# A preLN block (dilated attention, then a gMLP) rewritten: two token streams, 64-row tile pairs, GELU from table, a list-scheduled order

**Chip, cores, metric.** One core of a Trainium2 chip. The metric is device time in microseconds (us) of one execution. Each kernel ran four times on its chip, beside the kernel before; medians are quoted with their range.

## The reference, cut

```python
# x: [1, 2048, 448] bf16; 16 heads of 28; F = 1792, Fh = 896
def A(x, wqkv, wo):            # attention of 8 keys: positions s, s-2, ..., s-14
    q, k, v = split(x @ wqkv)
    logits = einsum(q, k[s - 2*j]) * 28**-0.5     # j = 0..7, masked below 0
    return (softmax(logits) @ v) @ wo
def B(x, w_in, w_sp, b_sp, w_out):
    z = gelu_tanh(x @ w_in)                       # [2048, 1792]
    z1, z2 = z[..., :896], layernorm(z[..., 896:])
    g = w_sp @ z2 + b_sp[:, None]                 # the "spatial" product, 2048 x 2048
    return (z1 * g) @ w_out
h  = x + A(layernorm(x), wqkv, wo)
h2 = h + B(layernorm(h), w_in, w_sp, b_sp, w_out)
```

## The kernel before

Contractions over 448 run as four passes of 112 rows. Attention takes tiles of 114 queries by 128 keys, of which the mask keeps every second key in a band. The GELU is built from arithmetic and a sigmoid, and the layernorms wait for all 16 blocks.

```python
def issue(self, exe, fn, reads=(), writes=(), prod=None, inc=1):
    ...                            # waits from what the resources hold
    self.ops[exe].append((waits, fn, prod, inc))   # EVERY instruction increments
...
def logits_block(b):               # 16 heads; four 32-row tiles side by side
    for g in range(4):
        for hh in range(4):
            iss("pe", lambda e, ...: e.matmul(out_ap, kT[hh*32:(hh+1)*32, g, t0:t0+nk],
                                qT[hh*32:(hh+1)*32, g, t0+PAD:t0+PAD+nq],
                                tile_position=(hh * 32, 0)), ...)
...
class GeluTile:                    # per 448 or 512 columns
    def copy(self):                # ACT: PSUM -> XB
        ... e.activation(self.XB, self.in_ps_ap, AF.Copy)
    def front(self):               # DVE x3
        ... e.tensor_tensor(self.WK, self.XB, self.XB, ALU.mult)
        ... e.tensor_scalar(self.WK, self.WK, GELU_C, 1.0, ALU.mult, ALU.add)
        ... e.tensor_tensor(self.WK, self.WK, self.XB, ALU.mult)
    def tanh(self):                # ACT
        ... e.activation(self.TB, self.WK, AF.Sigmoid, scale=GELU_K2)
    def back(self):                # DVE, with the row sum for z2
        ... e.tensor_tensor_reduce(self.out_dst_ap, self.TB, self.XB, 1.0, 0.0, ALU.mult, ALU.add, self.sum_x_ap)
    def sq(self):                  # ACT: sum of squares for the layernorm of z2
        ... e.activation(junk2[:, 0:self.n], self.out_dst_ap, AF.Square, accum_out=self.sum_sq_ap)
...
mean_var_from_sums(...); rstd3 = rsqrt_chain(...)   # after ALL 16 blocks of z2
for m in range(NB): ...                             # then normalise all of z2
```

The softmax here doesn't subtract the row's maximum and nothing guards it: scores larger than these inputs give would overflow.

## Time and profile before

| before | value |
|---|---|
| time, median (range) of the three runs the prediction had | 343.62 us (343.18 to 344.04) |
| time, median of the four runs beside the changed kernel | 343.83 us (343.18 to 344.11) |
| profiled span, mean granted TensorE clock | 342.4 us, 0.915 |
| busy: PE, DVE, ACT | 287.6, 242.8, 156.8 us |

The prediction shows the busy line, the slices and the stages. One more view: the page's costliest groups. Columns: line, engine, operation, output and input, shapes, count, then busy us, mean ns of one, and the idle time before with what ended it. These five lines are the arithmetic GELU, with 60 tiles each except the last, which is the 32 of z2:

```profile
L708 ACT ACTIVATE xb<-psum 128x448 bf16<-128x448 f32 (+1 forms) x60 | 33.4, 558 | 108.3 <-PE psum L755 95.5
...
L712 DVE TENSOR_TENSOR wk<-xb 128x448 bf16<-128x448 bf16 (+1 forms) x60 | 24.2, 404 | 40.1 <-ACT xb L708 40.1
...
L718 ACT ACTIVATE tb<-wk 128x448 bf16<-128x448 bf16 (+1 forms) x60 | 35.9, 598 | 12.7 <-DVE wk L714 12.7
...
L714 DVE TENSOR_TENSOR wk<-wk,xb 128x448 bf16<-128x448 bf16 (+1 forms) x60 | 24.5, 408 | 2.1
...
L723 DVE CUSTOM_DVE_ANT_0 z2p<-tb,xb 128x448 bf16<-128x448 bf16 x32 | 19.8, 618 | 0.9 <-ACT tb L718 0.8
```

A tile passes back and forth between ACT and DVE: 33.4 + 35.9 us of ACT and some 97 of DVE (with L713, 17.1, and L727, 11.7, not shown).

### The profile page before, as it was taken

The page shows a single profiled execution, that of the slowest core. Times are in us where ns is not written, and L with a number is a line of the kernel's source. Part 1 is how long each engine was busy: PE and PEld are TensorE (multiplying, and loading weights), DVE is VectorE, ACT ScalarE, POOL GpSimd, SP SyncE. Part 2 cuts the span into 40 slices and gives each one's busy share as a digit, 9 for nine tenths or more (in the row PEclk, how much of TensorE's full clock was granted, in tenths as well). Part 3 has the DMA queues.
Part 4 walks back from the last instruction along what each step waited for, and adds up shares of the span by engine and source line. Part 5 has one row for each costly group of instructions (what it writes and reads, how often), then busy time and mean ns, then how long its engine had stood idle before and what let it go on. Part 6 is the DMA issues. An engine that isn't in the chain of part 4 may idle for free.

```text
span 342.4 us, 4998 instructions
## 1 busy us (share of the span) xinstructions
PE 287.6 (84%) x1859; PEld 144.9 (42%) x1872; DVE 242.8 (71%) x670; ACT 156.8 (46%) x320; POOL 5.1 (1%) x17
## 2 busy tenths in 40 slices
PE   3789899999998848966550099999999999999996
PEld 1434455555565617521110034444444444444442
DVE  4987446897779779899999896554555565545554
ACT  1435878777866020899999322221222022212220
POOL 5000000000000000000000000000000000000000
PEclk9879989999987556999996589999999999999999
DMA  7999900000000069930000000001000100000001
GB/s 223 258 220 179 190 16 2 2 0 2 3 2 1 2 162 187 161 76 0 0 1 1 0 2 0 0 2 50 3 3 0 38 17 0 0 26 30 1 0 54
DMA packets 40537, 16.39 MB, mean 48 GB/s; under 512 B 34177, under 2 KB 39617, under 8 KB 40514
## 3 DMA queue, kind: packets, MB, share of 16 engines
q1 hardware_dynamic: 40514, 16.08, 22.5%
q8 instruction: 14, 0.23, 0.3%
q14 instruction: 9, 0.07, 0.1%
HBM read 5.85 MB, written 1.84 MB: 22 GB/s over the span
## 4 chain that ended last, share of the span: by engine, by line
PE 66%; DVE 28%; ACT 2%; issue 2%; DMA 1%; ACTq 0%; DVEq 0%
PE psum L800 29%; PE psum L383 9%; PE psum L755 7%; PE psum L823 6%; DVE z2p L723 5%; PE psum L400 4%; PE psum L485 4%; PE psum L444 4%; DVE wk L714 3%; DVE wk L712 3%; DVE wk L713 3%; DVE xhT L369 2%; DVE tring L351 2%; PE psum L416 2%; DVE st L347 1%
## 5 line engine op out<-in xcount | busy, mean ns | idle before, releaser
L708 ACT ACTIVATE xb<-psum 128x448 bf16<-128x448 f32 (+1 forms) x60 | 33.4, 558 | 108.3 <-PE psum L755 95.5
L800 PE MATMUL psum<-wspT_lo,z2p 128*128 128x512 bf16 x217 | 52.7, 388 | 17.9 <-DVE z2p L787 17.4
L712 DVE TENSOR_TENSOR wk<-xb 128x448 bf16<-128x448 bf16 (+1 forms) x60 | 24.2, 404 | 40.1 <-ACT xb L708 40.1
L800 PE MATMUL psum<-wspT_hi,z2p 128*128 128x512 bf16 x218 | 49.7, 379 | 0.3
L423 ACT ACTIVATE E<-psum 128x456 bf16<-128x456 f32 (+1 forms) x72 | 39.6, 550 | 15.1 <-PE psum L472 8.8
L800 PEld LDWEIGHTS psum<-wspT_lo,z2p 128*128 128x128 bf16 x224 | 21.9, 98 | 46.9 <-DVE z2p L787 22.3
L718 ACT ACTIVATE tb<-wk 128x448 bf16<-128x448 bf16 (+1 forms) x60 | 35.9, 598 | 12.7 <-DVE wk L714 12.7
L744 PE MATMUL psum<-w_in,xhT 112*128 112x448 bf16 x128 | 28.7, 365 | 11.1 <-ACT xb L708 11.1
L800 PEld LDWEIGHTS psum<-wspT_hi,z2p 128*128 128x128 bf16 x224 | 21.9, 98 | 26.5
L755 PE MATMUL psum<-xhT,w_in 112*128 112x512 bf16 x112 | 28.8, 379 | 1.2 <-ACT xb L708 1.2
L714 DVE TENSOR_TENSOR wk<-wk,xb 128x448 bf16<-128x448 bf16 (+1 forms) x60 | 24.5, 408 | 2.1
L744 PEld LDWEIGHTS psum<-w_in,xhT 112*128 112x128 bf16 x128 | 11.4, 101 | 28.0 <-ACT xb L708 19.0
L444 PEld LDWEIGHTS psum<-V,E 128*114 128x114 bf16 (+1 forms) x288 | 21.4, 149 | 2.4 <-issue 0.4
L823 PE MATMUL psum<-w_out,z1p 128*128 128x448 bf16 x112 | 22.0, 353 | 0.1
L444 PE MATMUL psum<-V,E 128*114 128x29 bf16 (+1 forms) x288 | 21.7, 210 | 0.0
L485 PE MATMUL psum<-wo,OT 112*128 112x448 bf16 x64 | 18.4, 420 | 3.9 <-DVE OT L475 2.8
L432 DVE TENSOR_TENSOR E<-E,maskb 128x1824 bf16<-128x1824 bf16 (+1 forms) x18 | 19.9, 1103 | 1.8 <-ACT E L423 1.7
L813 DVE TENSOR_TENSOR ub<-psum,bb 128x512 bf16<-128x512 f32 x28 | 19.1, 683 | 2.3 <-PE psum L800 2.3
L723 DVE CUSTOM_DVE_ANT_0 z2p<-tb,xb 128x448 bf16<-128x448 bf16 x32 | 19.8, 618 | 0.9 <-ACT tb L718 0.8
L383 PE MATMUL psum<-xhT,wqp 112*128 112x512 bf16 x64 | 18.1, 440 | 2.3 <-DVE xhT L369 2.3
L827 DVE TENSOR_TENSOR tring<-psum,x_tm 128x448 bf16<-128x448 f32 x16 | 10.0, 624 | 13.5 <-PE psum L823 13.5
L713 DVE TENSOR_SCALAR wk<-wk 128x448 bf16<-128x448 bf16 (+1 forms) x60 | 17.1, 285 | 2.1
(82 smaller groups left out, 338.1 us busy)
## 6 DMA issues: line engine op xcount, KB each, us to landing
x_tm<-in_A_x_dram SPq DMA_DIRECT2D x4, 448.0 KB, 7.2
out_dram<-tring SPq DMA_DIRECT2D x16, 112.0 KB, 1.7
w_in<-in_B_w_in_dram SPq DMA_DIRECT2D x1, 1568.0 KB, 15.5
stg<-in_A_wqkv_dram SPq DMA_DIRECT2D x1, 1176.0 KB, 9.9
w_out<-in_B_w_out_dram SPq DMA_DIRECT2D x1, 784.0 KB, 4.5
wo<-in_A_wo_dram SPq DMA_DIRECT2D x1, 392.0 KB, 12.9
wspT_lo<-in_B_w_sp_dram SPq DMA_TRANSPOSE x16, 4.0
wspT_hi<-in_B_w_sp_dram SPq DMA_TRANSPOSE x16, 4.1
```

The lines of the kernel that those rows point to most:

```text
L383: e.matmul(out_ap, wsrc[:, c, gg, :], xhT[0:DC, c, col0:col0 + 512], start=(c == 0), stop=(c == NCH - 1)),
L423: iss("act", lambda e, in_ap=in_ap, out_e=out_e: e.activation(out_e, in_ap, AF.Exp, scale=SCALE), reads=[r_bank[hh]], writes=[r_E[slot]])
L444: e.matmul(psum[0:nq, ob + h * 32: ob + h * 32 + DH + 1], E[0:nk, slot, eidx, 0:nq], V1[0:nk, vslot, h, 0:DH + 1]),
L708: iss("act", lambda e: e.activation(self.XB, self.in_ps_ap, AF.Copy), reads=[self.rbank], writes=[r_xb[s]])
L712: iss("dve", lambda e: e.tensor_tensor(self.WK, self.XB, self.XB, ALU.mult), reads=[r_xb[s]], writes=[r_wk[s]])
L714: iss("dve", lambda e: e.tensor_tensor(self.WK, self.WK, self.XB, ALU.mult), reads=[r_wk[s], r_xb[s]], writes=[r_wk[s]])
L718: iss("act", lambda e: e.activation(self.TB, self.WK, AF.Sigmoid, scale=GELU_K2), reads=[r_wk[s]], writes=[r_tb[s]])
L723: iss("dve", lambda e: e.tensor_tensor_reduce(self.out_dst_ap, self.TB, self.XB, 1.0, 0.0, ALU.mult, ALU.add, self.sum_x_ap), reads=[r_tb[ ...
L744: iss("pe", lambda e, c=c: e.matmul(out_ap, xhT[0:DC, c, PAD + 128 * m: PAD + 128 * m + 128], w_in[:, c, FH + D * k: FH + D * (k + 1)], st ...
L755: iss("pe", lambda e, c=c: e.matmul(out_ap, w_in[:, c, fc * 128:(fc + 1) * 128], xhT[0:DC, c, PAD + 512 * tc: PAD + 512 * (tc + 1)], start ...
L800: iss("pe", lambda e, sbk=sbk: e.matmul(out_ap, z2p[:, sbk, fc * 128:(fc + 1) * 128], wsrc[:, sbk, coff:coff + 512], start=(sbk == 0), sto ...
L823: iss("pe", lambda e, fc=fc: e.matmul(out_ap, z1p[:, fc, 128 * m:128 * m + 128], w_out[:, fc, :], start=(fc == 0), stop=(fc == FC7 - 1)), ...
```

## The change

The intent: fewer PE passes, no arithmetic GELU, and no stage in which PE waits for row statistics. Tokens 0..1023 lie on partitions 0..63 and tokens 1024..2047 on 64..127, so a contraction over 448 is seven passes of 64 rows for both streams, as tile pairs. Attention is split by parity (every second position), so a tile is 64 keys by 58 queries with a narrow band. Row sums are matmuls against ones, their reciprocal is exp of minus log on ACT. The reciprocal root is POOL's power, unit by unit. A list scheduler in the kernel, with estimated durations, fixes each engine's order; the exp and log of attention and the GELU alternate in six table phases.

```diff
 # matmuls of the contractions, here q/k: the two streams as 64-row tiles
+for c in range(NC7):
+    for s in range(2):
+        iss("pe", lambda e, ...: e.matmul(psum[:, bk[s]*512 + ...],
+            wp[64*s:64*s+64, c, cb:cb+128], xh[64*s:64*s+64, c, off+t0:off+t0+cw], ...))
-for c in range(NCH):
-    iss("pe", lambda e, ...: e.matmul(out_ap, wsrc[:, c, gg, :], xhT[0:DC, c, col0:col0+512], ...))
 # logits of one attention tile: 64 small matmuls, eight tiles of the array at a time
+for sg in range(8):
+    s, g = sg // 4, sg % 4
+    for w in range(2):                       # parity
+        for hh in range(4):
+            iss("pe", lambda e, ...: e.matmul(
+                psum[64*w:64*w+64, lb[hh]*512 + sg*JW : ... + JW],
+                kT[32*hh:32*hh+32, s, g, a+w:a+w+127:2],
+                qT[32*hh:32*hh+32, s, g, a+w:a+w+2*JW-1:2],
+                tile_position=(32*hh, 64*w)), ...)
 # (weighted V: likewise 64 matmuls of 64x32 tiles)
 # GELU
+iss("act", lambda e: e.activation(z2p[:, b, :]..., pair_view(zb, 2*s, D), AF.Gelu_apprx_tanh, accum_out=...))
-... copy / front / tanh / back as above
 # reciprocal root of a unit's variance
+iss("pool", lambda e: e.tensor_scalar(dst, var, EPS, None, ALU.add), ...)
+iss("pool", lambda e: e.tensor_tensor(dst, dst, nh, ALU.pow), ...)
 # order
+EPOCHS = [SET_E, SET_G, SET_E, SET_G, SET_E, SET_G]
+EP_TILE[i] = 0 if i < 4 else (2 if i < 7 else 4)     # attention tiles
+EP_UNIT[u] = 1 if u < 2 else (3 if u < 5 else 5)     # z2 units
+pl = Planner({"ps": range(8), "tr": range(NTR), "E": range(NE), ...}, EPOCHS, table_task)
+w_in, wsp loads: issued from the start, in order, on one queue
```

## The prediction

> **What bounds the kernel now.** I read the page's busy line and its 40 slices first, to see whether one engine carries the whole span.
>
> ```profile
> PE 287.6 (84%) x1859; PEld 144.9 (42%) x1872; DVE 242.8 (71%) x670; ACT 156.8 (46%) x320; POOL 5.1 (1%) x17
> ...
> PE   3789899999998848966550099999999999999996
> ...
> DVE  4987446897779779899999896554555565545554
> ACT  1435878777866020899999322221222022212220
> ```
>
> It doesn't: PE is full in slices 5 to 14 and from 23 on, but from 14 to 22 (120 to 195 us) it is half idle while DVE and ACT read 9. So I cut the span by stage (columns: length, then busy us and instructions of PE, PEld, DVE, ACT, POOL, then granted clock, DMA share, GB/s).
>
> ```profile
> 0.00:14.50 14.50, 7.60 (x28) 3.01 (x28) 9.17 (x33) 4.00 (x7) 5.06 (x17) 1.00 0.91 238
> 14.50:36.00 21.50, 18.70 (x97) 9.47 (x98) 17.85 (x62) 10.08 (x18) 0.00 (x0) 0.84 1.03 203
> 36.00:122.00 86.00, 79.81 (x882) 49.43 (x881) 61.62 (x141) 56.96 (x107) 0.00 (x0) 0.87 0.10 18
> 122.00:136.00 14.00, 8.53 (x70) 6.61 (x70) 13.28 (x51) 2.39 (x4) 0.00 (x0) 0.62 0.98 202
> 136.00:196.00 60.00, 30.35 (x136) 11.85 (x135) 55.03 (x189) 53.12 (x131) 0.00 (x0) 0.87 0.24 37
> 196.00:342.40 146.40, 142.59 (x651) 64.57 (x663) 85.86 (x199) 30.28 (x54) 0.00 (x0) 0.99 0.04 13
> ```
>
> Start; first q/k; attention (PE); the second layernorm as a barrier (DVE 13.3 of 14.0); the z2 half of the GELU (DVE 55.0 and ACT 53.1 of 60, PE half idle: there a tile takes four DVE passes and three of ACT); then z1, the spatial product and the output product, PE 142.6 of 146.4. The wait list shows what the layernorm of z2 then costs, one wait of PE for the normalised tensor, and the chain shows the pure PE rhythm afterwards:
>
> ```profile
> PE psum L800 <- DVE z2p L787: 17.4, 1, 17.4
> ```
>
> ```profile
> 202.38 0.87 PE psum L755 x4
> 203.25 3.46 PE psum L800 x16
> ```
>
> 16 matmuls of 512 columns in 3.46 us are 216 ns each, back to back.
>
> **What the Trainium skill says.** "TensorE: Matmul & The Clock Gate", section Back-to-back issue gap, gives N/2.4 + 2.5 ns at full clock; 216 ns for 512 columns agrees, and the 112-row matmuls above (L755, 0.87 us for four) take no less. So a contraction of 448 costs four passes of 112 rows now, and seven half passes of 64 rows, if two run side by side, cost 3.5. The same page, Part 3 (Packing small matmuls), says tiles in different row groups run together, some 4 ns apart. The trace agrees for 32-row tiles (columns: start, us, engine):
>
> ```profile
> 62.46 0.38 PE L416 MATMUL psum<-qT,kT 32*128 32x114 bf16 x16
> 62.77 0.41 PE L472 MATMUL psum<-ident,otm 114*112 114x114 bf16 x4
> ```
>
> 16 logits matmuls take 0.31 us to the next group's start, 19 ns each; alone they would be 114/2.4 + 2.5 = 50. 64-row pairs are shown by no run yet. "ScalarE: Activation LUTs", sections on what happens in an ACTIVATE and What ACT_TABLE_LOAD costs, gives 186 + 0.833 N ns for every function (the 456-column exp here took 551 ns, formula 566), so one GELU from table costs what one copy does, and 1283 ns a table load plus about 1380 of drain. The load is here too, 1283 ns, but the chain puts it at 139.06 and the next ACTIVATE at 140.35: no drain. "TensorEngine Tiling (Array Packing)", Key Properties, says a change of tiling mode drains the array; no view of the kernel before isolates this, so I treat it as a risk.
>
> **The change part by part.** *PE.* At full clock, columns/2.4 + 2.5 ns, the kernel before needs: q/k 128x216 = 27.6 us; V 72x189 = 13.6; attention output product 64x189 = 12.1; z2 128x189 = 24.2; z1 112x216 = 24.2; spatial 448x216 = 96.8; output 112x189 = 21.2; transposes 128x56 + 72x50 = 10.8; logits 288x19 = 5.6; weighted V 288x52 (8 in 0.39 us in the timeline, weights loads of 114 columns) = 15.1. Sum 251.2. After: q/k 7x4x(1024+1038) columns in 280 pair steps = 24.8; V 63 steps = 11.9; attention output unchanged 12.1; z2 112 pair steps 21.2; z1 98 = 21.2; spatial 96.8; output 21.2; transposes 231, two side by side, 6.5; per attention tile of 114 queries and both streams, logits 64 and weighted V 64 matmuls of 58 columns in eights, which I put at 0.6 each (8 steps of 25 to 75 ns), and row sums 0.25, so 9x1.45 = 13.1. Sum 228.8: 22 us less. No transposes of the attention output are left.
>
> *DVE*, with 155 ns + 1.04 per fp32 PSUM element (512 took 683, 448 took 624): LN1 17x0.81 + 16x0.32 + evictions 8x0.61, about 24.5; k evictions 8304 columns in 9 pieces 10.1; mask 9x1.12 (1824 elements took 1.105) = 10.1; attention scaling 9x1.10 = 9.9 (before 0.62+0.26+0.39 for each of 18); residual 8x1.09 = 8.7; LN2 23.4; statistics of z2 for six blocks 8.6; normalising z2 16x0.506 = 8.1; then gate 28x(0.683+0.424) = 31.0 and output 10.0. Sum 144, against 242.8. *ACT*: repack 5.0, q 8.3, V 8.4, exp 18x0.96 = 17.3, reciprocal as log and exp 17.3, z2 GELU 16.8 with its sums, squares of ten blocks 10x1.12 = 11.2, z1 GELU 14x1.04 = 14.5, six table loads 7.7: 107, against 157.
>
> *Barriers.* Row statistics now go block by block, with the power on POOL, so LN2, z2 and its layernorm are woven into attention. What lies there before z1 may start: PE 87 us, DVE 103, ACT 92. z1 and the spatial product are released when the last attention tile's exponentials are done, T8. Of the work before that, some 18 us of DVE (residual, LN2 and statistics of the last two units), 12 of ACT and 12 of PE come after T8. So T8 needs 85 us of DVE, 80 of ACT and 75 of PE. DVE starts at 4 us (the first x landed at 4.1), loses about 4 waiting for x behind q/k/v weights that are now loaded twice (2.4 MB for 1.2, at the 203 to 238 GB/s above about 12 us), and with three engines alternating in a chain of eight steps a tile I give it 88%: 8 + 85/0.88 = 105 us.
>
> *Path after T8.* PE has z1 21.2, z2 of three units 8.0, output product and transposes of the last units 4, spatial 96.8, output 21.2: 151 us. DVE (18+41) and ACT (12+14.5) fit beside it. 3% of stalls, as in the last stage of before (142.6 of 146.4), add 4, the last add and store 3 to 4. 105 + 151 + 4 + 4 = 264.
>
> So of 80 us gained, about 22 are shorter PE work and about 58 idle PE time, chiefly the 60 us GELU stage and the two layernorm barriers.
>
> **Rivals.** (a) PE takes over from the start: if DVE and ACT keep up, time is first products at 13 us, 229 of PE, 3 of tail: 245. For it: no engine's sum before z1 exceeds 103; against: the DVE sum alone is more than PE's 87 there. (b) The woven stage runs worse than 88%: eight PSUM banks serve logits (4 at a time), z2 (4), pairs everywhere (2), only two exponent buffers, and table phases forbid GELU while exponentials run; order is fixed ahead of time, so each mis-estimate is a wait. At 72% T8 is 126 and the time 285. The PE clock may help it along: where PE idled before (122 to 136) it was granted 0.62, and half a clock for all 75 us of PE work would make PE the bound, T8 about 155 and the time near 314. Against: at half-busy 136 to 196 the clock was still 0.87. (c) 64-row pairs don't run side by side: q/k, V, z2, z1 cost twice, 79 us more, about 335; the 19 ns of the 32-row tiles speaks against it. (d) POOL's power on one or two columns is slow (no view of before has one; its smallest operations took 146 ns): latency a unit, hidden except at the end; 3 to 8 us.
>
> **Range and chances.** (a) and (b) give the ends; I take the middle of them weighted to my sum: 264, 8 in 10 within 250 to 283. Only (c) or a clock held low throughout comes near 337; faster 0.96.
>
> **What would show it.** The changed profile should show DVE about 145 busy, ACT about 105; no stretch with PE under half after 20 us; the last exponentials at 100 to 112; from there PE over 95% with 16-matmul spatial groups still 3.46 us; z1's groups of 14 matmuls about 1.51 us (7 steps of 216 ns), where 3.0 would prove (c); before T8, DVE over 80% busy and PE clock mostly above 0.85. It is wrong if PE or ACT, not DVE, fills the stage before T8, if table switches or bank waits open gaps over 3 us in all three engines, or if the end after T8 is much longer than 159.

## The result, and the profile after

**304.04 us median of four runs (301.42 to 304.49), against 343.83: ratio 0.8845 (95% interval 0.879 to 0.8899).** A ratio here is the mean time of one kernel's fast runs over that of the other's of the same rounds, so it is not quite the ratio of the medians. The change is faster, but 40 us slower than the 264 predicted and outside the range. The outputs are correct. Executions over 1.5% slower than the fastest of the same kernel are left out of the means.

The page's busy line and slices of the changed kernel (40 slices of 7.6 us, busy tenths):

```profile
PE 274.6 (91%) x3324; PEld 156.5 (52%) x3335; DVE 141.0 (47%) x258; ACT 101.8 (34%) x126; POOL 47.3 (16%) x134
...
PE   8398786999688998997988999999999999999996
...
DVE  3576644677347468666465401332422242234233
ACT  1345313525775655786755861000000000000000
...
PEclk9667956999999799997899999999999999999999
```

DVE (141, predicted 144) and ACT (101.8, predicted 107) came as summed. PE did not: 274.6 for 228.8. And PE stands at 6 to 9 from the third slice on: there is no idle stage left, but PE is the busiest engine all the way. The clock row shows stretches at 5 to 7 tenths before slice 20.

The same cut by stage as before, at the end of the last attention tile's exponentials, which the prediction calls T8. The last of them is the exp of the reciprocal; the softmax exps of that tile end at 139.9, and everything below uses the later one (columns: length, then busy us and count of PE, PEld, DVE, ACT, POOL, clock, DMA share, GB/s):

```profile
0.00:14.30 14.30, 7.73 (x37) 3.28 (x37) 5.59 (x15) 3.25 (x4) 7.88 (x30) 0.85 0.96 183
14.30:145.80 131.50, 115.43 (x2418) 83.01 (x2420) 79.52 (x143) 73.62 (x90) 28.84 (x72) 0.88 0.42 74
145.80:302.60 156.80, 151.47 (x871) 70.21 (x878) 55.87 (x101) 24.97 (x33) 10.62 (x32) 1.00 0.21 48
```

This one view locates the miss. After T8 the kernel takes 156.8 us, predicted 159. T8 itself is 145.8, predicted 105. In the stage before it DVE is busy 60% (79.5 of 131.5), and PE 88%.

Which PE work grew? The page's groups:

```profile
L946 PE MATMUL psum<-xh,w_in 64*128 64x512 bf16 x196 | 21.9, 375 | 0.0
...
L763 PE MATMUL psum<-reg 32*64 32x58 bf16 x576 | 15.1, 195 | 3.7 <-issue 1.9
...
L804 PE MATMUL psum<-reg 64*32 64x58 bf16 x576 | 16.9, 191 | 0.9 <-ACT z2p L899 0.9
```

L946 is z1: 21.9 us for 196 matmuls, predicted 21.2. One of them takes 375 ns from start to end, yet one starts every 110 ns, so the 64-row pairs do run side by side. L763 (logits) and L804 (weighted V) were put at 9 x 0.6 = 5.4 us each and take 15.1 and 16.9.

From the records of the trace I summed PE's time from each matmul's start to the next one's, by line. It divides 274.6 us into 243.3 at full clock and 31.3 at half. What lies above the prediction's terms, both clocks together: weighted V 10.8, logits 9.2, q/k 7.6, warm-up matmuls 6.1 (left out of my sum), transposes 4.7, V 3.9, z2 2.4, output product of attention 0.9. Of q/k, V and transposes, 22 us were at half clock.

The timeline of PE shows one group each (columns: start, us, engine, line, count):

```profile
67.32 1.52 PE L735 MATMUL psum<-reg,xh 64*64 64x448 bf16 x28
68.77 1.51 PE L763 MATMUL psum<-reg 32*64 32x58 bf16 x64
70.21 0.58 PE L603 MATMUL psum<-ident,tring 128*64 128x128 bf16 x14
```

The 64 logits matmuls hold PE from 68.77 to 70.21, 1.44 us, at full clock. Inside such a group most of the first 30 or so start 3 to 4 ns apart, the others some 34.5 ns apart. It is not the clock that paces them; what does is asked below.

### The profile page after: what moved, and what is told of

It reads as the page before. It is cut to its first block, busy times and chain, and to the rows that moved or that the text cites. A ratio compares the mean times of both kernels' runs of the same rounds, so it can differ in the third digit from the quotient of the medians.

```text
span 302.6 us, 7388 instructions
## 1 busy us (share of the span) xinstructions
PE 274.6 (91%) x3324; PEld 156.5 (52%) x3335; DVE 141.0 (47%) x258; ACT 101.8 (34%) x126; POOL 47.3 (16%) x134
## 4 chain that ended last, share of the span: by engine, by line
PE 79%; DVE 5%; POOL 4%; ACT 4%; issue 3%; DMA 3%; SPq 1%; POOLq 0%; ACTq 0%; DVEq 0%
PE psum L983 32%; PE psum L694 10%; PE psum L886 7%; PE psum L1012 7%; PE psum L946 5%; PE psum L735 4%; PE psum L804 4%; PE psum L763 4%; DMA x_tm<-in_A_x_dram 3%; PE psum L603 3%; PE psum L867 2%; ACT z2p L899 2%; POOL rs L570 2%; DVE st L579 1%; PE psum L792 1%
## 5 line engine op out<-in xcount | busy, mean ns | idle before, releaser
L993 DVE TENSOR_TENSOR ub<-psum,reg 128x512 bf16<-128x512 f32 x28 | 19.4, 692 | 74.0 <-PE psum L983 74.0
L983 PE MATMUL psum<-reg,z2p 128*128 128x512 bf16 x218 | 48.5, 379 | 0.3
L694 PE MATMUL psum<-xh,reg 64*128 64x256 bf16 (+2 forms) x560 | 33.4, 279 | 7.7 <-issue 3.3
L983 PEld LDWEIGHTS psum<-wspT_lo,z2p 128*128 128x128 bf16 x224 | 21.9, 98 | 26.5 <-issue 0.4
L983 PEld LDWEIGHTS psum<-reg,z2p 128*128 128x128 bf16 x224 | 22.0, 98 | 26.3
L694 PEld LDWEIGHTS psum<-xh,reg 64*128 64x128 bf16 x560 | 25.8, 106 | 13.8 <-issue 3.9
L886 PE MATMUL psum<-w_in,xh 64*128 64x448 bf16 x224 | 24.0, 357 | 4.6 <-DVE reg L713 1.7
L579 DVE BATCH_NORM_STATS2 st<-x_tm 128x6 f32<-128x448 bf16 x32 | 19.6, 612 | 6.0 <-DMA x_tm<-in_A_x_dram 5.8
L946 PE MATMUL psum<-xh,w_in 64*128 64x512 bf16 x196 | 21.9, 375 | 0.0
L1012 PE MATMUL psum<-reg 128*128 128x448 bf16 x112 | 21.8, 352 | 0.0
L570 POOL TENSOR_TENSOR rs<-rs,nhalf 128x2 f32<-128x2 f32 (+1 forms) x32 | 20.6, 644 | 2.7
L611 DVE COPY xh<-psum 128x896 bf16<-128x896 bf16 x16 | 9.8, 616 | 20.4 <-PE psum L603 11.1
L763 PE MATMUL psum<-reg 32*64 32x58 bf16 x576 | 15.1, 195 | 3.7 <-issue 1.9
L804 PE MATMUL psum<-reg 64*32 64x58 bf16 x576 | 16.9, 191 | 0.9 <-ACT z2p L899 0.9
L804 PEld LDWEIGHTS psum<-reg 64*32 64x32 bf16 x576 | 16.1, 91 | 2.2 <-ACT z2p L899 1.4
L763 PEld LDWEIGHTS psum<-reg 32*64 32x64 bf16 x576 | 13.6, 108 | 6.8 <-issue 2.9
L956 ACT ACTIVATE reg<-psum 128x1024 bf16<-128x1024 f32 x14 | 14.2, 1021 | 6.6 <-PE psum L946 6.5
## 6 DMA issues: line engine op xcount, KB each, us to landing
w_in<-in_B_w_in_dram SPq DMA_DIRECT2D x4, 784.0 KB, 12.1
```

The costliest lines, as they stand in the source:

```text
L570: iss("pool", lambda e: e.tensor_tensor(dst, dst, nh, ALU.pow), reads=rr + [r_nhalf], writes=rr)
L579: iss("dve", lambda e: e.bn_stats(st[:, b, :], x_tm[:, b, :]), reads=[r_x[b]], writes=[rl[b]])
L694: iss("pe", lambda e, c=c, s=s, gi=gi, lhs=lhs: e.matmul(psum[:, bk[s] * 512 + cw * gi:bk[s] * 512 + cw * gi + cw], lhs, xh[64 * s:64 * s ...
L763: iss("pe", lambda e, s=s, g=g, sg=sg, w=w, hh=hh: e.matmul(psum[64 * w:64 * w + 64, lb[hh] * 512 + sg * JW:lb[hh] * 512 + sg * JW + JW], ...
L804: iss("pe", lambda e, w=w, hh=hh, s=s, g=g, sg=sg: e.matmul(psum[32 * hh:32 * hh + 32, ob[w] * 512 + sg * JW:ob[w] * 512 + sg * JW + JW], ...
L886: iss("pe", lambda e, c=c, k=k, s=s: e.matmul(psum[:, zb[2 * s + k] * 512:zb[2 * s + k] * 512 + D], xh[64 * s:64 * s + 64, c, HALO + 128 * ...
```

## The experiments

**Theories.** For the slow small matmuls: *increments* (each of the 64 increments PE's semaphore, and increments take their turn; *R2*); rival *R1*, *columns* (58 columns through eight tiles take that long); and *S*, *supply* (the instructions come no faster than one pair of weight load and matmul in 34.5 ns). For the rest of the late T8: *phases* (*P*: exp and GELU forbid each other; its rival *B*: banks and other waits set the stage); *C*, *clock* (small matmuls and waits drop the granted clock); *F*, *fetch* (PE's own instructions arrive late beside bulk loads).

The experiments were compared with the kernel before in the same rounds. Here are all, with T8 and what follows it, from each profiled run. In the last column a matmul's time runs from its start to the next one's.

Two cautions. The runs fall into five sets, each on its own chip (e1 to e4; e5 to e8; e9 to e11; e12 to e14; e15), so across sets only ratios compare. And T8 comes from one profile a kernel, while runs of one kernel differ: the change's four runs took 304.3, 304.5, 303.8 and 301.4 us at a granted clock of 0.938, 0.938, 0.938 and 0.954. So I take a difference of T8 of about 3 us for nothing.

| run | median (range), us | ratio to before (95%) | T8 | after T8 | PE before T8 from 14.3 us: full / half clock / idle |
|---|---|---|---|---|---|
| the change | 304.04 (301.42–304.49) | 0.8845 (0.879–0.8899) | 145.8 | 156.8 | 86.1 / 29.3 / 16.0 |
| e1_half (wrong output) | 290.41 (287.54–290.50) | 0.8418 (0.8358–0.8478) | 130.8 | 158.0 | 71.8 / 21.8 / 23.0 |
| e2_wide (wrong output) | 300.52 (296.81–304.64), two runs slow | none | 140.2 | 156.1 | 96.5 / 12.8 / 16.6 |
| e3_one_increment | 294.26 (290.92–295.71) | 0.8517 (0.844–0.8595) | 134.6 | 157.7 | 75.2 / 21.2 / 24.0 |
| e11_every_second_increment | 294.11 (291.50–295.66) | 0.8574 (0.8505–0.8644) | 136.5 | 157.5 | 81.0 / 21.7 / 19.6 |
| e8_one_increment_wide (wrong output) | 294.93 (293.81–295.39) | 0.862 (0.8574–0.8667) | 135.8 | 157.6 | 75.6 / 22.5 / 23.6 |
| e5_no_phases (exp in place of a GELU) | 289.99 (289.00–290.76) | 0.8479 (0.8433–0.8525) | 132.8 | 154.5 | 75.0 / 23.5 / 20.2 |
| e6_replanned | 287.70 (287.02–290.57) | 0.8442 (0.8376–0.8508) | 131.6 | 153.6 | 75.2 / 19.9 / 21.6 |
| e7_phases_moved | 285.43 (284.51–286.38) | 0.8348 (0.8301–0.8394) | 123.9 | 158.8 | 72.7 / 17.4 / 19.6 |
| e9_loads_spread | 300.82 (299.14–302.56) | 0.8762 (0.8687–0.8836) | 142.7 | 158.1 | 89.8 / 23.5 / 15.0 |
| e10_moved_and_spread | 286.14 (281.09–288.89), two runs slow | 0.8253 (0.8155–0.8351) | 126.1 | 159.9 | 71.8 / 19.0 / 21.1 |
| e12_loads_held | 297.22 (296.89–300.05) | 0.8739 (0.8668–0.8811) | 137.0 | 158.2 | 93.6 / 16.6 / 12.5 |
| e13_one_increment_loads_held | 288.81 (288.19–290.97) | 0.8486 (0.8422–0.8549) | 128.8 | 157.7 | 77.6 / 16.8 / 20.2 |
| e14_all_mended | 280.17 (279.73–285.04) | 0.8208 (0.8132–0.8285) | 121.6 | 157.3 | 72.2 / 16.9 / 17.7 |
| e15_w_in_early | 275.98 (275.01–278.07) | 0.8107 (0.8023–0.8191) | 118.1 | 156.1 | 73.7 / 15.1 / 14.3 |
| e4_before_gelu_table | 314.67 (313.70–315.05) | 0.9138 (0.909–0.9186) | – | – | – |

### The small matmuls: half of them, wider ones, one increment, every second increment

**e1_half** issues every second of the logits and weighted V matmuls at twice the columns (the output is wrong).

```diff
-for sg in range(8):
+for sg in range(0, 8, 2):          # each writes 2*JW columns
```

> Wrong result on purpose: half as many logits and weighted-V matmuls, each of 116 columns instead of 58, so the array streams the same columns. Theory S (supply: PE runs what waits in its queue, 32 weight-load-and-matmul pairs, at the array's speed, and gets further pairs only about every 34.5 ns): a group of 32 comes from the queue, and logits and weighted V fall from 14.6 and 16.2 us in all to 4 to 8 each; the last exponentials end at 118 to 130 instead of 146 and the time is 278 to 290. Rival R1 (the array is the limit, column tiles do not run side by side): groups keep their time, 300 to 306. Rival R2 (each matmul's semaphore increment costs some 26 ns in line): groups halve, about 288 to 292, so this run alone does not part S from R2.

**e2_wide** keeps 64 matmuls and gives them 104 columns for 58.

```diff
-psum[..., sg*JW : sg*JW + JW],                qT[..., a+w : a+w+2*JW-1 : 2]
+psum[..., sg*JW : sg*JW + 104] (as 2 x 52),   qT[..., a+w : a+w+103 : 2] broadcast twice
```

> Wrong result on purpose: the same number of logits and weighted-V matmuls, each of 104 columns instead of 58. S: the pairs past the first 32 of a group come at 34.5 ns whatever their columns, so a group goes from about 1.6 to at most 1.9 us and the time stays within 298 to 308. R1: group times grow by 104/58, 14.6 and 16.2 us become 26 and 29, and the time about 328. R2: no change either. If windows of low array activity are what halves the clock, more columns should also take away one or more of the half-clock windows (37.5 us in all at half now).

**e3_one_increment** (correct) buffers the matmuls of one scheduled task and lets only the last increment; the last one takes over the reads and writes of all. Others wait for that last one, which is sound if PE's matmuls finish in order; the outputs stayed correct.

```diff
+def flush(self):
+    g, self.grp = self.grp, None
+    for fn, reads, writes in g[:-1]:
+        self.issue("pe", fn, reads, writes, prod="none")     # no increment
+    self.issue("pe", g[-1][0], union_of_reads, union_of_writes)
```

> Correct result: only the last matmul of each group increments the semaphore, all else equal. S: nothing changes, logits and weighted V keep 24 to 29 ns a matmul, 300 to 306 us. R2: they fall to under 12 ns each and the time to 285 or less.

**e11_every_second_increment** does the same in pairs of matmuls, so that half the increments stay.

```diff
+for k in range(0, len(g), 2):      # only the second of two increments
```

> Correct result: every second matmul increments the semaphore, a dose between the changed kernel (64 in a logits group, 1.32 us from first to last start) and one increment (0.50 us). If each increment costs about 23 to 27 ns in line: 0.7 to 0.9 us a group, 295 to 301 us. If the number does not matter as long as some matmuls do not increment: 0.50 us, 292 to 296.

Measured from a group's first start to its last, median of the groups that ran wholly at full clock, logits / weighted V: the change 1.32 / 1.54 us, e1 0.22 / 0.40 (32 matmuls), e2 1.35 / 1.55, e11 0.91 / 1.03, e3 0.50 / 0.48. The timeline of PE in e3, where logits are L783:

```profile
65.67 1.52 PE L755 MATMUL psum<-reg,xh 64*64 64x448 bf16 x28
67.12 0.70 PE L783 MATMUL psum<-reg 32*64 32x58 bf16 x64
67.76 1.36 PE L623 MATMUL psum<-ident,tring 128*64 128x128 bf16 x28
```

Against the changed kernel's 68.77 to 70.21, the same 64 matmuls hold PE for 0.64 us and not 1.44. In e11's timeline it is 63.75 to 64.77, 1.02 us.

What follows. Columns (R1) fell with e2: nearly twice the columns, the same time for a group (its two fast runs took 296.8 and 298.0 us in all, for a reason taken up under the clock). Supply (S) had been my favourite, for the 34.5 ns looked like a fetch rate; e3 issues the very same stream of loads and matmuls in less than half the time, so it fell too. e1 alone could not have told supply from increments, as it halves both.

Increments are shown, by taking them away and by their dose: 1, 32 and 64 increments give 0.64, 1.02 and 1.44 us. The starts inside a group show the price of one. In the later half of it they are 34 to 35 ns apart in the change, 8 to 9 ns in e3, and in e11, where every second matmul increments, 34 to 35 and 8 ns by turns: some 26 ns for an increment. Over the whole group that is 13 ns each in the mean, as most of the first 30 or so starts are not spread in any of the three; why, no run tells. e3 takes the increments from every task of PE, not from these two lines alone. The time fell by some 10 us (ratio 0.8845 to 0.8517) and T8 by 11.2. The two lines' busy time fell by 17.8 us (15.1 + 16.9 to 7.3 + 6.9), so some 7 us of it turned into waiting.

Both whole times missed what was expected: e3 took 294.26 us for 285 or less, e11 294.11 for 295 to 301. In whole time the two can't be told apart; the dose shows in the groups alone. The stages of e3 show the waiting:

```profile
14.30:134.60 120.30, 96.27 (x2416) 63.05 (x2413) 78.23 (x143) 72.59 (x89) 28.48 (x72) 0.90 0.46 81
134.60:292.40 157.80, 153.12 (x881) 70.46 (x875) 55.83 (x101) 25.00 (x34) 10.62 (x32) 0.99 0.20 47
```

PE is busy 96.3 of 120.3 us before T8, and the fullest of the others, DVE, is at 65% (78.2). Something more holds T8 back.

### What is left of the gain: the GELU alone

**e4_before_gelu_table** puts one part of the change into the kernel before: one GELU ACTIVATE per tile (with the sum), and the squares on DVE. The rest of that kernel, stages and barriers, stays.

```diff
-copy: activation(XB, psum, AF.Copy);  front: 3 DVE passes;  tanh: activation(Sigmoid);  back: DVE
+copy: activation(out_dst, psum, AF.Gelu_apprx_tanh, accum_out=sum_x);  front, tanh, back: nothing
-sq: activation(junk2, out_dst, AF.Square, accum_out=sum_sq)
+sq: dve tensor_tensor_reduce(junk2, out_dst, out_dst, ..., sum_sq)
```

> The kernel before with one part of the change alone: GELU as one table activation out of PSUM, with the sum of squares on DVE. Theory: the 60 us stage of z2 becomes bound by PE (128 matmuls of 189 ns, 24 us) or by DVE's sums (32 x 0.70 = 22 us) and ends 28 to 33 us earlier, the rest keeps its time: 308 to 318. Then most of what the rewrite gained is the table's. Rival: the gain of the rewrite is from weaving the stages together, and this alone gives under 15 us: over 328.

Measured 314.67 us against 345.13 in those rounds: 30 us, as expected. Its stages, to be held against the last three before (14.0, 60.0 and 146.4 us long):

```profile
122.00:136.00 14.00, 8.58 (x73) 7.66 (x73) 13.26 (x49) 2.94 (x5) 0.00 (x0) 0.54 1.03 223
136.00:166.00 30.00, 24.77 (x130) 12.52 (x128) 24.48 (x87) 21.11 (x66) 0.00 (x0) 0.99 0.40 62
166.00:312.80 146.80, 143.60 (x664) 64.62 (x664) 47.25 (x87) 15.53 (x26) 0.00 (x0) 0.99 0.04 13
```

The z2 stage shrinks from 60 to 30 us and the others do not move, although DVE in the last one drops from 85.9 to 47.3: that was off the path. So the table GELU by itself, put into the old kernel, gains 30 of the rewrite's 40 us. All the rest (streams, pairs, parity, weaving) then adds about 10, where my predicted gain of 80 left some 50 for it. It removes the two layernorm stages, and gives much of that back in the longer stage before T8.

### Phases, estimates and order

**e5_no_phases** (on e3) lets exponentials stand for the GELU of z2, so that no table phase orders attention and z2. The check called the output correct, so its tolerance does not see this term; I count it as a changed function all the same.

```diff
-EPOCHS = [SET_E, SET_G, SET_E, SET_G, SET_E, SET_G];  AF.Gelu_apprx_tanh (z2)
+EPOCHS = [SET_E, SET_G];                              AF.Exp (z2)
```

> Wrong result on purpose: one increment a group as in the run before, and exp in place of GELU for z2, so that no table phase separates z2 from the attention tiles (five of the six table loads and all the phase gates before z1 are gone; the order of work follows). Theory P (the phases hold up the woven stage: a tile's exponentials may not start until the GELUs of the phase before are done): the last exponentials end 7 to 15 us earlier than the 134.6 of the run with one increment, time 278 to 288 against 294. Rival B (bank and dependency waits set the stage whatever the phases): within 4 us of it, 290 to 297.

**e6_replanned** (on e3) gives the scheduler durations as measured in the traces and frees the banks of logits and z2 pair by pair.

```diff
-"rs", pool 0.2;  "rs3", pool 0.8 or 0.2;  "tT", pe 0.45;  "mml"/"mmo", pe 0.45
+"rs", pool 1.15; "rs3", pool 2.3 or 1.0;  "tT", pe 0.65;  "mml"/"mmo", pe 0.6
-tx[1].rel = [("ps", lb)]
+tx[0].rel = [("ps", Part(lb, 0, 2))];  tx[1].rel = [("ps", Part(lb, 2, 4))]
```

> Correct result: one increment a group, the order planned with the durations that the trace showed (logits and weighted-V group 0.6, transposes 0.65, POOL's two operations for a reciprocal root 1.15, 2.3 with sums, attention scaling 1.26), and the banks of logits and z2 given back pair by pair. If the order suffered from wrong durations: last exponentials at 122 to 131, time 280 to 290. If not: as with one increment alone, 291 to 297.

**e7_phases_moved** (on e6) puts one more attention tile into the first exponential phase and moves one z2 unit from the second GELU phase to the last, and changes priorities (and the engine that repacks q) with it.

```diff
-EP_TILE: 0 if i < 4 ...;  EP_UNIT: 1 if u < 2, 3 if u < 5;  TU = 11.0; switch penalty 2.0
+EP_TILE: 0 if i < 5 ...;  EP_UNIT: 1 if u < 2, 3 if u < 4;  TU = 10.5; switch penalty 0.5
```

> Correct result: as the replanned one, and the table phases cut at tiles 5 and 7 and units 2 and 4 (before: 4 and 7, 2 and 5), with a few priorities changed. If P holds: last exponentials at 114 to 125, time 272 to 284, the fastest of all. Under B no better than the replanned one.

Without phases T8 comes 1.8 us earlier than in e3 (132.8 against 134.6, where P had it 7 to 15 earlier), and the ratio, 0.8479 for 0.8517, lies within the other's interval: no gain is shown, and the phases as such were not the wait in this order. Estimates: e6 takes T8 to 131.6, at a ratio of 0.8442, whose interval also overlaps that of e3, so its gain isn't shown either. The move of the phases with its priorities takes T8 to 123.9, as P expected; the stages of e7:

```profile
14.30:123.90 109.60, 89.92 (x2399) 63.18 (x2401) 76.81 (x140) 71.69 (x87) 24.63 (x62) 0.90 0.51 89
123.90:282.80 158.90, 156.05 (x910) 71.92 (x904) 57.96 (x106) 27.93 (x39) 13.58 (x40) 0.98 0.20 47
```

Here most of what T8 gains comes back after it: 153.6 to 158.9 us after T8, since z2 moved behind it, so the time falls by only 2.3 (ratio 0.8442 to 0.8348; the intervals just overlap; 272 to 284 was expected). T8 is not the goal by itself. e7 changes several things at once; which of them did it, no run tells.

### The clock

**e8_one_increment_wide** is e3 with e2's wide matmuls.

```diff
 e3's flush
+e2's 104 columns
```

> Wrong result on purpose: one increment a group, and logits and weighted-V matmuls of 104 columns instead of 58. Theory C (a window of some 3.4 us in which the array does little is followed by one at half clock, and the short matmuls are such windows): groups keep 0.5 to 0.6 us, but the time at half clock falls from 30.7 us to under 22, the last exponentials come 3 to 7 us before 134.6, time 286 to 292. Rival (the clock follows idle time alone): half clock stays at 28 to 33 us, time within 2 us of 294.

In e2, half-clock time in the whole run fell from 37.5 to 17.1 us, and T8 to 140.2, although the groups took as long: more columns per matmul seemed to keep the clock up (C). With one increment it did not: 30.7 us in e8 and in e3. So the rule "more columns, higher clock" is not confirmed. Nor was e2's high clock steady: its four runs were granted 0.970, 0.970, 0.944 and 0.955. What the traces show is only that the granted clock is 1 or 0.5, in pieces that are multiples of some 3.4 us. But for e2, half-clock time is lowest where the loads are held (23.9 us in e12, e13 and e14, 20.5 in e15), yet e9, which kept the longer stall, was granted 0.943 in its profiled run and 0.954 to 0.955 in the other three, against 0.949 to 0.960 in e12. So that the stalls bring on the half clock is not shown. Its cause stays open.

### PE's instructions

In the changed kernel PE stands still twice for no wait that the profile shows. The wait list has both as "issue" (us in total, times, longest; the other, on L763, is 1.9 us long), and the timeline shows the longer one:

```profile
PE psum L694 <- issue: 3.3, 1, 3.3
```

```profile
35.08 0.58 PE L603 MATMUL psum<-ident,tring 128*64 128x128 bf16 x14
35.60 0.39 PE L694 MATMUL psum<-xh,reg 64*128 64x256 bf16 x4
39.29 2.74 PE L694 MATMUL psum<-xh,reg 64*128 64x256 bf16 x24 [3.30 <-issue]
```

It breaks in the middle of a row of like matmuls that all have their operands. Counted over all that the trace has of PE (matmuls, weight loads and waits), the gap stands before PE's instruction 961, and the second (1.9 us) before 1217: 256 apart. The trace has pieces of 16,384 bytes on the instruction queue; those that began at 19.7 and 24.1 us were followed by the next only at 36.2, right inside the gap, and the one after that began at 45.7, just before the second gap; from there to 79 us they are 4.5 to 6.3 us apart. Meanwhile the w_in and spatial weights were being loaded, as the transfers of 28 to 42 us show:

```profile
DMA packets 1635, 2.86 MB, mean 204 GB/s; under 512 B 48, under 2 KB 1634, under 8 KB 1634
...
q8 instruction: 1, 0.02, 0.6%
```

One instruction piece in 14 us, beside 2.8 MB of weights. The Trainium skill, "Runtime: NRT & Kernel Launch", section Instruction fetch mechanics, says that each engine fetches its program in 16 KiB blocks of 256 instructions over a queue of its own, with the cost "mostly hidden". Block and count agree with this trace (16,384 bytes, 256 instructions between gaps). Here it isn't hidden.

**e9_loads_spread** (the change) and **e10_moved_and_spread** (e7) reorder those loads among the scheduled work, with dependencies for the scheduler only.

```diff
-ld_wsp(b, 0, 3.0 + 0.01 * n)                        # for all 16 blocks
+ld_wsp(b, 0, 3.0 + 0.01 * n, deps=[AFTER[n]])       # order only: no wait comes of it
```

> Correct result: the changed kernel with one thing altered, when its bulk loads start: the z1 half of w_in and the 16 transposing loads of the spatial weights wait for stages of the attention instead of following each other from 20 to 55 us. Theory F (PE's own instructions come in pieces of 16 KB, 256 instructions, over the same DMA engines, and in the full stretch a piece comes late: the changed kernel's PE stood 3.3 us at 36.0 us and 1.9 us at 46.3 us before instructions 961 and 1217, with no wait on them): those two gaps vanish, half clock falls by one or two windows of 3.4 us, time 293 to 300 against 304. Rival: the gaps have another cause and stay, time within 2 us of 304.

> Correct result: the kernel with one increment a group, replanned and its phases moved (285.4 us; its PE stood 4.0, 4.0, 2.0 and 1.1 us before instructions 961, 1217, 1729 and 2753, 11 us in all), with the loads spread. F: those gaps shrink to under 3 us in all, last exponentials at 110 to 118 instead of 123.9, time 271 to 279. Rival: other waits take the time up, 282 to 287.

These two failed as tests: the dependencies ordered the loads but made none wait, so the row of loads began at 27.0 us, as before (26.8), with only one of w_in moved to 47.8. In e9 the gap before instruction 961 stayed (3.29 us); in e10, whose profile fell in a slow run, there were gaps of 1.65 and 6.63 us. They say nothing about fetch.

**e12_loads_held** (the change) and **e13_one_increment_loads_held** (e3) make each load wait in truth, by reading what the work before it writes.

```diff
-ld_win(1, 0, "sp", 2.0)
+ld_win(1, 0, "sp", 2.0, deps=[t_ot[0]], after=[r_OT[0]])     # after= adds reads=, so a wait
+ld_wsp(b, 0, ..., deps=[AFTER[n][0]], after=[AFTER[n][1]])
```

> Correct result: the changed kernel, all compute instructions in the same order, but w_in and the transposing loads of the first half of the spatial weights now really wait (each reads a result of the attention; in the run with spread loads they kept their old start, since the order alone gave no wait). F (PE's instructions come late through a full set of DMA engines): the gaps before instructions 961 and 1217, 3.3 and 1.9 us, shrink to under 1 us each, time 292 to 300. Rival: the gaps stay, 301 to 305.

> Correct result: one increment a group and the loads held, order as in the changed kernel. Its gaps without the hold were 5.0 us before 1217 and 2.2 before 1473. F: under 1 us each, last exponentials at 122 to 130 instead of 134.6, time 281 to 289 against 294. Rival: 291 to 296.

In e12 both gaps are gone. The same place in its timeline:

```profile
32.16 0.58 PE L603 MATMUL psum<-ident,tring 128*64 128x128 bf16 x14
32.68 1.71 PE L694 MATMUL psum<-xh,reg 64*128 64x256 bf16 x28
34.31 0.58 PE L603 MATMUL psum<-ident,tring 128*64 128x128 bf16 x14
```

28 matmuls of that line run through in 1.71 us, where 3.30 us of stall lay in the middle. Instruction pieces now begin at 19.7, 23.4, 28.0 and 33.3 us. One gap of 1.25 us, before instruction 2241, is new. T8 came at 137.0 for 145.8, and the half-clock time fell from 37.5 to 23.9 us in the run. In whole time e12 (0.8739) can't be told from e9 (0.8762), which kept the stall. In e13, whose base e3 stood 4.97 us before 1217 and 2.16 before 1473, the first of these is gone and the second has grown:

```profile
37.16 2.79 PE L714 MATMUL psum<-xh,reg 64*128 64x256 bf16 x47
44.06 1.25 PE L714 MATMUL psum<-xh,reg 64*128 64x256 bf16 x9 [4.11 <-issue]
```

It stands before instruction 1473, again a multiple of 256 after 961, at the time when the held w_in load ran, and its piece began at 41.25 us, inside the gap. e13 (0.8486) can't be told from e3 in time. But the stall goes with the load: it left 961 and 1217 when the load was held back, and (e15 below) leaves 1473 when the load is taken from there. That is fetch, shown by moving the load twice; what the pieces queue behind inside the DMA engines, the trace doesn't tell.

**e14_all_mended** is e7 with the held loads; **e15_w_in_early** is e14 with the z2 half of w_in loaded before wo and not held.

```diff
-ld_win(1, 0, "sp", 2.0, deps=[t_ot[0]], after=[r_OT[0]])
+ld_win(1, 0, "sp", 0.98)                             # likewise (1, 1)
```

> Correct result: one increment a group, replanned, phases moved, loads held. F: the gaps before 961, 1217, 1729 and 2753 (11 us in all) go, last exponentials at 110 to 118, time 269 to 278. Rival: 282 to 287.

> Correct result: as the last one, but the z2 half of w_in is loaded ahead of wo, before 30 us, instead of after the first attention tile. There the load of w_in between 33 and 45 us stood beside a new gap of 5.5 us before instruction 1473. F: that gap goes (no bulk load then) or moves to 20 to 32 us if the pieces fall into the earlier load; last exponentials 116 to 121 against 121.6, time 274 to 280. Rival: the gap stays at 38 to 44 us, time 279 to 282.

e14 has 5.48 us of stall before instruction 1473; in e15, with that load gone from there, it is gone as well, and gaps of 0.78, 0.85, 0.82 and 2.20 us before 1729, 2241, 2497 and 2753 stay. PE's order of work is the same in e7, e14 and e15, so the three show what the late pieces cost. All such gaps of over 0.7 us come to 11.1 us in e7, 8.7 in e14 and 4.7 in e15, T8 to 123.9, 121.6 and 118.1: 6.4 us less of gaps, 5.8 less of T8. (e14 was expected at 269 to 278 us and its rival at 282 to 287; 280.17 is neither. e15 came as expected.) e15's stages:

```profile
14.30:118.60 104.30, 89.27 (x2409) 63.13 (x2411) 77.63 (x142) 72.64 (x89) 25.71 (x62) 0.92 0.51 94
118.60:274.20 155.60, 152.03 (x889) 70.89 (x894) 57.66 (x106) 27.34 (x38) 13.85 (x40) 1.00 0.20 48
```

275.98 us, ratio 0.8107 (0.8023 to 0.8191): correct, faster than both kernels, 19% under the kernel before. PE is busy 86% before T8, DVE 74%: even here PE is the fuller engine.

## Why the prediction was wrong, point by point

- **The path after T8: right.** Predicted 151 + 4 + 4 = 159 us, measured 156.8; PE busy 151.5 of it (97%), and 153.6 to 159.9 in every experiment.
- **DVE and ACT sums, 64-row pairs: right.** DVE 141.0 for 144, ACT 101.8 for 107, z1 at 110 ns a matmul. Rival (c) is refuted. No stretch of PE under half after 20 us: held.
- **"Logits 64 and weighted V 64 matmuls of 58 columns in eights, which I put at 0.6 each": wrong.** The groups take 1.32 and 1.54 us from first to last start, because each matmul increments the semaphore. With a single increment it is 0.50 us: the figure was right for the matmuls without their increments, and I had left out what the program adds to them. I had cited Part 3 of "TensorE: Matmul & The Clock Gate" for tiles side by side, and that same part has the section "The cost: per-tile semaphore tail", which says that increments serialise, and that one on the last tile is enough. The kernel before gave no warning: in the group that I read (19 ns a matmul) four start 3 to 4 ns apart and the next four 41 to 51 ns later, which is the pace of 114 columns (the prediction's own formula gives 50), not that of increments. Taking the increments away gave 11 us of T8 and some 10 of the time (e3).
- **"T8 needs 85 us of DVE, 80 of ACT and 75 of PE": wrong in PE.** My PE total of 228.8 was 274.6. Counting half-clock time at half (an estimate), PE in the changed kernel does 86.1 + 29.3/2 = 101 us of full-clock work between 14.3 us and T8, and in e3 75.2 + 21.2/2 = 86. Warm-up was left out of the sum, and the other lines' excess is not split further. There is a slip in the sum besides: its own terms before z1 (24.8, 11.9, 12.1, 21.2, 6.5, 13.1) add to 89.6 and not 87, so 75 should have been about 78.
- **"I give it 88%: 8 + 85/0.88 = 105": wrong, for it takes DVE as the bound.** DVE was 60% busy. PE was the fuller engine, at 88%: 115.4 us of work for the 75 of the sum, 29 of them at half clock, and 16 of standing still, of which 5.2 were the two stalls of its instruction stream and the rest waits of up to 1.9 us each, most of them for DVE and ACT. The prediction's own sign of error, "if PE or ACT, not DVE, fills the stage before T8", came true. Rival (b) had the right direction (T8 126 to 155) but not the cause: what it named, banks and table phases, gave little when the phases were taken away (e5), and the moved cut came with other changes (e7). Rival (a) had PE as the bound, but with the same small PE sum, at 245. Rival (d), the slow power on POOL, is there (575 to 712 ns each; DVE waits for POOL 7.5 us at L593 and 14.2 at L932 in all), but no run isolates what it costs.
- **Clock.** I put its loss at nothing in the 264. It was 29 us at half clock before T8, some 15 us of work if half the clock is half the pace (an estimate). e12 removes the stalls of 3.3 and 1.9 us and has 13.6 us less of half clock, but the change's own runs differ by some 10 (granted clock 0.938 to 0.954 over some 300 us). The cause stays open.
- **Instruction fetch: not thought of.** The rewrite has 7,388 instructions for 4,998, with 6,659 matmuls and weight loads for 3,731, and moves the big loads beside them.

The steps from 145.8 to e15's 118.1 in T8 add up so: increments 11.2 (e3), estimates and banks 3.0 (e6), phases and priorities 7.7 (e7), loads held and w_in early 5.8 (e14, e15). The 3.0 is within what single profiles differ by. Some 13 us to the predicted 105 remain; in e15 PE is still idle for 14.3 us and at half clock for 15.1 before T8, and the runs do not explain these further.

## What to carry to other kernels

When a rewrite trades few large matmuls for many small ones, cost the instruction itself (its increment, its fetch), not only the array: let the last of a group increment, and keep bulk loads from running beside a dense instruction stream (here a block of 256 every 4 to 6 us). Before crediting a large change, try its simplest part alone in the old kernel: one function swapped gave 30 us here, where the whole change gave 40. And an engine whose sum "fits" isn't the bound if another's sum is wrong: recompute all of them at the durations, clock included, that the first trace shows.

## What the Trainium skill lacked or had wrong

- "TensorE: Matmul & The Clock Gate", Part 3, per-tile semaphore tail: it gives 26.3 ns an increment as a tail after the last matmul. The price agrees (34.5 ns between starts with an increment, 8 to 9 without), but here it showed as spacing inside a group of 64, in its later half, where the page has a tail behind it. The advice, one increment on the last, held. For eight tiles at 58 columns with one increment, later starts were 8 to 9 ns apart, where the page's span model adds about 4 ns a tile.
- "Runtime: NRT & Kernel Launch", Instruction fetch mechanics: "mostly hidden". Beside bulk loads a block of 256 PE instructions came late and PE stood 3.3 and 1.9 us (the change), 4.1 (e13), 5.5 (e14).
- "ScalarE: Activation LUTs", What ACT_TABLE_LOAD costs: the load's 1283 ns agree, the drain of about 1380 ns does not show (load at 139.06, next ACTIVATE at 140.35 in the kernel before).
- No page that I found has a duration for POOL's power on a column or two: here 575 ns for 128x1 and 712 for 128x2, beside 273 to 304 for the addition before it; the scheduler had 0.2 us for both together.
- The clock: "TensorE: Matmul & The Clock Gate", Part 1, has the two levels, full and half, as the traces do. Its table ties the half clock to an idle window of some 3.4 us, and a later section to frequent short idles between groups; here PE ran 29 us at half clock before T8 with 16 us of idle in all, no gap there over 3.3 us. The page gives no figure for the latter, and the runs did not settle which activity counts.
